# The first microseconds of an attention and gated-layer kernel: w_in loaded by row halves, contiguous copies of turned q, copies of turned k over two banks

## Chip, cores and metric

The kernel runs on one core of a Trainium2 chip. The metric is the device time of one execution in microseconds (us), as the median of several executions; the profile's span is some 1.8 us shorter than that time.

## The reference

```python
def attention(q, k, v):              # 8 batches, 8 heads, 576 tokens, 64 wide; chunks of 64 tokens
    scores = q_chunk @ k_chunk.T / 8
    return softmax(scores) @ v_chunk
def layers(x, w_in, w_out, beta):    # x: 4608 tokens x 512; w_in 512 x 2048; w_out 2048 x 512
    h = x @ w_in
    return (h * sigmoid(beta * h)) @ w_out
# x is the attention's output with the heads side by side
```

## The kernel before

The work is cut into nine blocks of 512 tokens. In a block q and k are cast to bf16 and turned, TensorE forms scores of 64 by 64, ScalarE the exponentials (E), TensorE the product with v, VectorE the normalized x (`x_sb`), which is turned to `xT`. Then follow the first layer (16 tiles of 128 features, tile t in PSUM bank t % 4 of F), tanh and product (`tt`, `g`), and the second layer. The attention of a block is woven into the second layer of the block before it. Blocks 0 and 1 turn q, k and x on TensorE and copy them out of PSUM; from block 2 on transposing transfers issued by SyncE do it. Each engine runs its own list in the order of the times given to `at(...)`.

The parts that the argument touches (cuts marked with `# ...`):

```python
def load_w_in(e0, n):                       # 256 columns of w_in, all 512 rows: runs of 1 KB
    a = w_in[:, 256 * e0:256 * e0 + 256 * n].rearrange("(c p) f -> p c f", p=128)
    # ... issued by SyncE into wstage

def turn_half(blk, name, half, ps, bank, eng):          # blocks 0 and 1
    mid = ps[:, bank, :].bitcast(BF16)
    for i in range(8):
        # ... TensorE turns cast[name][:, c:c + 128] into mid[:, 128 * i:128 * i + 128]
    copy(eng, turned[name][:, :, 256 * half:256 * half + 256].rearrange("x h (p i) -> x h p i", i=8),
         mid.rearrange("x (i p h) -> x h p i", i=8, h=4), ...)      # 1024 elements, read at a step of 4

def scores_half(blk, half, bank0):                      # 32 matmuls of 64 columns
    # ...
    e.matmul(A[64 * c2:64 * c2 + 64, bank0 + h2, col:col + 64],
             turned["k"][r, hp, t], turned["q"][r, hp, t])          # t: 64 neighbouring elements

def exp_half(blk, half, h2, bank0):
    P.op("act", lambda e: e.activation(E[:, 2 * half + h2, :], A[:, bank0 + h2, :], AF.Exp, scale=0.125), ...)

def turn_x(blk, m):                                     # blocks 2 and later
    P.dma("sp", lambda e: e.dma_start_transpose(xT[:, :, 128 * m:128 * m + 128], x_sb[:, m, :]), ...)

at(-99.2, spin, 11, A, 3)                               # warming matmuls, 512 columns each
# ... block 0: tiles 0 and 1 of the first layer in two halves of 256 tokens, tile 2 and later whole
```

The softmax here doesn't subtract the row's maximum and nothing guards it: scores larger than these inputs give would overflow.

Of the kernel before, what the change touches and what calls it, by code (L numbers as in the profile page):

```python
# [11 lines left out]
def K(*key, v=0):  # L12

    return key, v
# [144 lines left out]
def bass_chunk_attention__then__act_swish_beta_kernel(nc, q, k, v, w_in, w_out, beta, out):  # L159
# [7 lines left out]
    with ExitStack() as es:  # L167
# [64 lines left out]
        def halve_beta():  # L232
            for i in range(2):
                P.op("dve", lambda e, i=i: e.transpose(beta_turned[:, i, :], beta_raw[:, i::2]),
                     reads=[K("beta_raw", g) for g in range(4)], writes=[K("beta_turned", i)])
            P.op("pool", lambda e: e.tensor_single_scalar(
                beta_half[:, :, :], beta_turned[:, :, 0:8].rearrange("p i e -> p e i"), 0.5, ALU.mult),
                reads=[K("beta_turned", i) for i in range(2)], writes=[K("beta_half")])


        def load_w_in(e0, n):
            s, at = e0 // 2, 256 * (e0 % 2)
            w = 256 * n

            def f(e):
                a = w_in[:, 256 * e0:256 * e0 + w].rearrange("(c p) f -> p c f", p=128)
                return e.dma_start(
                    wstage[:, s, :].rearrange("p (c f) -> p c f", c=4)[:, :, at:at + w], a)
            P.dma("sp", f, writes=[K("ws", s, e, v=("i", e)) for e in range(e0 % 2, e0 % 2 + n)])

        def cast_w_in(e0, n, engines):
            s, at, w = e0 // 2, 256 * (e0 % 2), 256 * n
            per = 4 // len(engines)
            st = wstage[:, s, :].rearrange("p (c f) -> p c f", c=4)
            for i, eng in enumerate(engines):
                c = slice(per * i, per * i + per)
                dst, src = w_in_bf[:, c, 256 * e0:256 * e0 + w], st[:, c, at:at + w]
                r = [K("ws", s, e, v=("i", e)) for e in range(e0 % 2, e0 % 2 + n)]
                wr = [K("w_in", e0 + x, cc) for x in range(n) for cc in range(4)[c]]
                copy(eng, dst, src, r, wr)  # L260

        def copy(eng, dst, src, r, wr):
            if eng == "act":
                P.op("act", lambda e: e.activation(dst, src, AF.Copy), reads=r, writes=wr)
            else:
                P.op(eng, lambda e: e.tensor_copy(dst, src), reads=r, writes=wr)  # L266
# [75 lines left out]
            copy(eng, dst, src, [K(name + "stage", blk, 2 * half + j, 0, v=blk) for j in range(2)],  # L342
                 [K(name + "cast", 2 * half + j, v=blk) for j in range(2)])

        def turn_half(blk, name, half, ps, bank, eng):
            key = K(*pkey(ps, bank), v=("turn", blk, name, half))
            mid = ps[:, bank, :].bitcast(BF16)
            for i in range(8):
                c = 1024 * half + 128 * i
                P.op("pe", lambda e, i=i, c=c: e.transpose(  # L350
                    mid[:, 128 * i:128 * i + 128], cast[name][:, c:c + 128], identity[:, :]),
                    reads=[K("identity")] + [K(name + "cast", 2 * half + x, v=blk) for x in range(2)],
                    writes=[key])
            copy(eng, turned[name][:, :, 256 * half:256 * half + 256].rearrange("x h (p i) -> x h p i", i=8),
                 mid.rearrange("x (i p h) -> x h p i", i=8, h=4),
                 [key], [K(name + "T", hp, half, v=blk) for hp in range(4)])

        def scores_half(blk, half, bank0):
            for hp in range(4):
                for m in (2 * half, 2 * half + 1):  # L360
                    for h2, c2 in ((0, 0), (1, 1), (0, 1), (1, 0)):
                        col = (2 * hp + m % 2) * 64

                        def f(e, hp=hp, h2=h2, c2=c2, col=col, m=m):
                            r = slice(64 * h2, 64 * h2 + 64)
                            t = slice(64 * (2 * m + c2), 64 * (2 * m + c2) + 64)
                            return e.matmul(A[64 * c2:64 * c2 + 64, bank0 + h2, col:col + 64],
                                            turned["k"][r, hp, t], turned["q"][r, hp, t])
                        P.op("pe", f, reads=[K("qT", hp, half, v=blk), K("kT", hp, half, v=blk)],
                             writes=[K("A", bank0 + h2, v=("s", blk))])  # L370

        def exp_half(blk, half, h2, bank0):
# [3 lines left out]
        def pkey(ps, bank):  # L376
            return "A" if ps is A else "F", bank
# [22 lines left out]
        EB = wstage[:, 0, :].bitcast(BF16).rearrange("k (g x) -> k g x", x=128)  # L400

        def clear_E():
            P.op("pool", lambda e: e.memset(EB, 0.0), writes=[K("ws", 0, e, v="E") for e in range(2)] +
                 [K("EB", u, c2) for u in range(2) for c2 in range(2)])

        def exp(blk, u, c2):
# [79 lines left out]
        def gate(blk, t):  # L486
            bank, T, e0, i = t % 4, NT * blk + t, t // 2, t % 2
            P.op("act", lambda e: e.activation(tt[:, T % NTT, :], F[:, bank, :], AF.Tanh,  # L488
                                               scale=beta_half[:, e0, i:i + 1]),
                 reads=[K("F", bank, v=("h", T)), K("beta_half")], writes=[K("tt", T % NTT, v=T)])  # L490
            P.op("dve", lambda e: e.scalar_tensor_tensor(  # L491
                g2[:, t, :], tt[:, T % NTT, :], 1.0, F[:, bank, :], ALU.add, ALU.mult),
                reads=[K("F", bank, v=("h", T)), K("tt", T % NTT, v=T)], writes=[K("g", t, half, v=blk) for half in range(2)])


        def mm1_pair(blk, pair, half, bank, n, tiles=(0, 1)):
# [66 lines left out]
        def at(time, fn, *args):  # L563
            events.append((time, len(events), fn, args))
# [50 lines left out]
        at(-98.9, load_beta)  # L615
        for m in range(4):
            at(-97.9, load, 0, "v", m)
        at(-99.2, spin, 11, A, 3)
        for e0, n in [(i, 1) for i in range(6)] + [(6, 2)]:
            at(-97.7, load_w_in, e0, n)  # L620
        for j in range(4):
            at(-97.6, load_w_out, j)
        for half in range(2):
# [1 line left out]
                at(-97.5, load_half, 1, name, half)  # L625
        for m in range(4):
            at(-97.4, load, 1, "v", m)
        for t, name, half, cast_eng, turn_t, bank, eng in (
                (4, "q", 0, "dve", 4.7, 0, "act"), (4.1, "k", 0, "dve", 6, 1, "dve"),
                (6.5, "q", 1, "pool", 7.9, 2, "act"), (6.6, "k", 1, "dve", 8.3, 3, "dve")):  # L630
            at(t - 100, cast_half, 0, name, half, cast_eng)
            at(turn_t - 100, turn_half, 0, name, half, F, bank, eng)
        for half, t, t2 in ((0, 8, 8.05), (1, 9.7, 9.75)):
            at(t - 100, scores_half, 0, half, 2 * half)
            for h2 in range(2):
# [1 line left out]
        for m in range(4):  # L637
            at(m - 91.4 if m < 3 else -88.65, cast_v, 0, m, "pool" if m < 3 else "dve")
        for m, t, t2, ps, bank, xb, eng in ((0, 9.2, 11.1, F, 0, 2, "act"), (1, 10, 11.35, A, 0, 3, "act"),
                                            (2, 11.3, 13.5, A, 2, 2, "act"), (3, 12.6, 16.5, A, 0, 3, "dve")):  # L640
            for u in range(2):
                at(t - 100, attend, 0, m, u, ps, bank + u)
            at(t + 0.1 - 100, normalize, 0, m, (0, 1), ps, bank)
            at(t2 - 100, turn_x_pe, 0, m, F, xb, eng)
        for t, n, ps, bank in ((8.35, 2, F, 1), (10.5, 1, F, 3), (11.11, 2, F, 1), (11.4, 1, F, 1),
                               (12.9, 2, F, 1)):
            at(t - 100, spin, n, ps, bank)
        at(8.2 - 100, halve_beta)
        at(13 - 100, cast_w_in, 0, 1, ("pool", "act"))
        at(-83.2, cast_w_in, 1, 1, ("dve", "pool"))  # L650
        for e0 in range(2, 8):
            at(2 * e0 - 2.5, cast_w_in, e0, 1, ("pool", "pool"))
        for j in range(4):
            at(15 + 3 * j, cast_w_out, j, ("pool", "pool"))
        for name, half, ceng, tc, tt_, bank, eng in (
                ("q", 0, "dve", 24, 26.1, 0, "act"), ("k", 0, "dve", 25, 27, 1, "act"),
                ("q", 1, "pool", 26, 29, 2, "dve"), ("k", 1, "pool", 27, 29.9, 3, "act")):
            at(tc, cast_half, 1, name, half, ceng)
            at(tt_, turn_half, 1, name, half, A, bank, eng)
        for half, ts in ((0, 28.95), (1, 30.93)):  # L660
            at(ts, scores_half, 1, half, 2 * half)
            for h2 in range(2):
# [1 line left out]
        for m, ta, ps, bank, tx, xps, xb, eng in (  # L664
# [5 lines left out]
            at(ta + 0.01, normalize, 1, m, (0, 1), ps, bank)  # L670
            at(tx, turn_x_pe, 1, m, xps, xb, eng)

        at(40, clear_E)
        for blk in range(2, NB):
            prepare(blk, 32 * blk - 16)
            attention(blk, 32 * blk - 16)
        for blk in range(NB):
            for n in range(16):
                if n < (2, 6)[blk] if blk < 2 else False:
                    pair, half = (n % (1, 3)[blk], n // (1, 3)[blk])  # L680
                    a = (pair, half, n % 4, n)
                    for i in range(2):
                        at((-84 + 1.05 * i, -82.9)[n] if blk == 0 else 32 * blk + n, mm1_pair, blk, *a, (i,))
                    at((-82.95, 0.9)[n] if blk == 0 else 32 * blk + n + 0.88, gate_pair, blk, *a)
                else:
                    at(32 * blk + n, mm1, blk, n)
                    at(32 * blk + n + 0.05 + 0.9 * (blk == 1), gate, blk, n)
                s, part = (n // 4, n % 4) if blk else (n % 4, n // 4) if n < 8 else \
# [64 lines left out]
```

## Time and profile before

| | before |
|---|---|
| time, median (lowest to highest) | 290.38 us (290.19 to 291.29), 3 runs |
| span of the profiled run | 288.4 us |
| TensorE busy | 278.3 us, 96% of the span |
| second layer of block 0 starts | 31.52 us |
| each block from the third on | 29.49 us |

In the profile lines PE is TensorE, ACT ScalarE, DVE VectorE, POOL GpSimd and SP SyncE; a q behind the name (SPq, ACTq) is the engine's sequencer issuing a transfer; L with a number is a line of the kernel, x with a number how many instructions are taken together, and to turn is to transpose. An issue is the instruction that starts a transfer; the transfer lands later.

The lines that carry the prediction stand in it. Two stages that it does not show matter later. The first is the attention of block 1, woven into the second layer of block 0. This is TensorE's list of work there: start, us from the first start to the last end, line, what, count.

```profile
43.73 0.44 PE L367 MATMUL A<-qT,kT 64*64 64x64 bf16 x32
...
47.59 0.42 PE L367 MATMUL A<-qT,kT 64*64 64x64 bf16 x28
...
49.94 1.05 PE L499 MATMUL F<-xT,w_in_bf 128*128 128x256 bf16 x8
```

A group of 32 scores takes 0.44 us, and the first layer of block 1 begins at 49.94 us. The second stage is the hand-over of x in block 3: SyncE issues four transposing transfers from 101.53 us on, and TensorE goes from the second layer (L523) into the first layer (L479) with no break. SyncE's list, then the chain in order of time:

```profile
101.53 5.49 SPq L453 DMA_TRANSPOSE xT<-x_sb  x4
```

```profile
104.05 6.04 PE F L523 x28
110.09 2.16 PE F L479 x10
```

### The profile page before, as it was taken

What the parts mean: (1) busy time and instruction counts of PE and PEld (TensorE: products, weight loads), DVE (VectorE), ACT (ScalarE), POOL (GpSimd) and SP (SyncE); (2) the same over time, 40 slices, a digit from 0 to 9 for tenths busy, and PEclk for the clock granted to TensorE, in tenths of its full rate; (3) what the DMA queues carried; (4) which work ended last, traced back from release to release, by engine and by line L of the source; (5) the groups of instructions that cost most, each with busy time, mean ns of one, the idle gap of its engine ahead of it and who ended that gap; (6) DMA issues with size and microseconds to landing.
All of it is one profiled execution on the core that took longest, in us unless ns stands there. A gap on an engine that the chain in (4) does not pass through costs nothing.

```text
span 288.4 us, 5455 instructions
## 1 busy us (share of the span) xinstructions
PE 278.3 (96%) x2208; PEld 140.4 (49%) x2243; DVE 148.7 (52%) x292; ACT 161.5 (56%) x233; POOL 77.4 (27%) x115
## 2 busy tenths in 40 slices
PE   5899999999999999999999999999999999999995
PEld 1654456745444544455445544554445444544444
DVE  0777436784348444844384527451856185608601
ACT  2477326877167815882588247834783387438510
POOL 1436854823230622150206020410224020000000
PEclk9799999999999999999999999999999999999999
DMA  6999999999899999895999599958989990340033
GB/s 228 262 350 395 404 332 286 248 178 246 149 273 193 275 203 236 190 232 147 239 222 195 134 237 214 222 112 206 212 165 188 208 226 2 80 135 6 0 71 74
DMA packets 134183, 57.50 MB, mean 199 GB/s; under 512 B 116624, under 2 KB 126096, under 8 KB 134160
## 3 DMA queue, kind: packets, MB, share of 16 engines
q1 hardware_dynamic: 128560, 47.33, 74.4%
q10 hardware_dynamic: 5600, 9.84, 11.2%
q8 instruction: 17, 0.28, 0.4%
q14 instruction: 6, 0.05, 0.1%
HBM read 36.71 MB, written 9.44 MB: 160 GB/s over the span
## 4 chain that ended last, share of the span: by engine, by line
PE 87%; DMA 6%; SPq 3%; issue 1%; DVE 1%; POOL 1%; POOLq 0%
PE F L523 39%; PE F L479 36%; PE A L420 2%; PE F L499 2%; DMA kstage<-in_k_dram 2%; DMA vstage<-in_v_dram 2%; DMA qstage<-in_q_dram 2%; PE A L394 2%; PE F L548 1%; SPq L306 1%; SPq L287 1%; PE F L350 1%; SPq L453 1%; PE A L350 1%; SPq L333 1%
## 5 line engine op out<-in xcount | busy, mean ns | idle before, releaser
L491 DVE SCALAR_TENSOR_TENSOR g<-tt,F 128x512 bf16<-128x512 bf16 x136 | 93.5, 687 | 71.5 <-ACT tt L488 71.3
L523 PE MATMUL F<-w_out_bf,g 128*128 128x512 bf16 x542 | 124.9, 379 | 1.7 <-issue 1.0
L479 PE MATMUL F<-xT,w_in_bf 128*128 128x512 bf16 x527 | 117.9, 379 | 0.9
L488 ACT ACTIVATE tt<-F,beta_half 128x512 bf16<-128x512 f32 x136 | 93.4, 687 | 24.5 <-PE F L479 24.3
L479 PEld LDWEIGHTS F<-xT,w_in_bf 128*128 128x128 bf16 x544 | 53.1, 98 | 64.1 <-DVE g L491 0.5
L523 PEld LDWEIGHTS F<-w_out_bf,g 128*128 128x128 bf16 x560 | 52.1, 98 | 57.3 <-POOL w_out_bf L266 0.3
L531 ACT ACTIVATE ostage<-F 128x512 f32<-128x512 f32 x33 | 19.6, 598 | 67.1 <-PE F L523 66.9
L266 POOL CAST vaug<-vstage 128x512 bf16<-128x512 f32 x35 | 21.5, 613 | 75.9 <-DMA vstage<-in_v_dram 72.1
L415 ACT ACTIVATE wstage<-A 64x1024 bf16<-64x1024 f32 x28 | 28.5, 1018 | 5.2 <-PE A L394 4.7
L266 POOL CAST qcast<-qstage 128x1024 bf16<-128x1024 f32 (+1 forms) x18 | 17.0, 945 | 44.8 <-DMA qstage<-in_q_dram 44.2
L446 DVE TENSOR_TENSOR x_sb<-A,rden 128x256 bf16<-128x256 f32 (+1 forms) x62 | 27.9, 450 | 2.1
L444 DVE RECIPROCAL rden<-A 128x4 f32<-128x4 f32 (+1 forms) x62 | 11.1, 179 | 30.6 <-PE A L420 29.4
L266 POOL CAST kcast<-kstage 128x512 bf16<-128x512 f32 (+1 forms) x29 | 18.1, 628 | 25.1 <-DMA kstage<-in_k_dram 24.8
L420 PEld LDWEIGHTS A<-vaug,wstage 128*128 128x128 bf16 x224 | 10.8, 98 | 6.6
L420 PE MATMUL A<-vaug,wstage 128*128 128x65 bf16 x224 | 11.7, 193 | 0.0
L266 POOL CAST w_in_bf<-wstage 128x512 bf16<-128x512 f32 x14 | 8.2, 613 | 7.5 <-DMA wstage<-in_moe_w_in_dram 7.5
L266 POOL CAST w_out_bf<-wstage 128x1024 bf16<-128x1024 f32 x8 | 8.1, 1040 | 1.9 <-DMA wstage<-in_moe_w_out_dram 1.9
L266 DVE CAST qcast<-qstage 128x1024 bf16<-128x1024 f32 x2 | 1.9, 934 | 12.6 <-DMA qstage<-in_q_dram 12.6
L499 PE MATMUL F<-xT,w_in_bf 128*128 128x256 bf16 x64 | 8.0, 273 | 0.2
L509 ACT ACTIVATE tt<-F,beta_half 128x256 bf16<-128x256 f32 x16 | 6.7, 470 | 2.2 <-PE F L499 2.1
L553 DVE TENSOR_SCALAR ostage<-F 128x256 f32<-128x256 f32 x2 | 0.8, 424 | 12.0 <-PE F L548 12.0
L513 DVE SCALAR_TENSOR_TENSOR g<-tt,F 128x512 bf16<-128x512 bf16 x8 | 5.5, 686 | 2.2 <-ACT tt L509 2.2
(58 smaller groups left out, 88.8 us busy)
## 6 DMA issues: line engine op xcount, KB each, us to landing
vstage<-in_v_dram SPq DMA_DIRECT2D x32, 256.0 KB, 5.2
out_dram<-ostage ACTq DMA_DIRECT2D x32, 256.0 KB, 3.4
kstage<-in_k_dram SPq DMA_DIRECT2D x30, 256.0 KB, 6.5
qstage<-in_q_dram SPq DMA_DIRECT2D x12, 512.0 KB, 5.4
wstage<-in_moe_w_out_dram SPq DMA_DIRECT2D x4, 1024.0 KB, 12.9
wstage<-in_moe_w_in_dram SPq DMA_DIRECT2D x6, 512.0 KB, 8.1
qstage<-in_q_dram SPq DMA_DIRECT2D x8, 256.0 KB, 8.6
wstage<-in_moe_w_in_dram SPq DMA_DIRECT2D x1, 1024.0 KB, 11.0
```

The costliest lines, as they stand in the source:

```text
L266: P.op(eng, lambda e: e.tensor_copy(dst, src), reads=r, writes=wr)
L415: P.op("act", lambda e: e.activation(dst, src, AF.Exp, scale=0.125), reads=[K("A", 2 * u + i, v=("s", blk)) for i in range(2)], writes=[K( ...
L420: P.op("pe", lambda e, h=h: e.matmul(A[:, bank, 128 * (h % 4):128 * (h % 4) + 65], EB[:, 16 * u + 8 * (h % 2) + 4 * (h // 2 % 2) + m, :], ...
L444: P.op("dve", lambda e: e.reciprocal(rd, o[:, :, :, 64]), reads=r, writes=[K("rden", m, u, v=blk) for u in us])
L446: P.op("dve", lambda e: e.tensor_tensor(x_sb[:, m, 256 * us[0]:256 * (us[0] + n)].rearrange("p (b h d) -> p b h d", h=4, b=n), o[:, :, :, ...
L479: P.op("pe", lambda e, c=c: e.matmul(F[:, bank, :], w_in_bf[:, c, 256 * e0 + i:256 * e0 + 256:2], xT[:, c, :], start=(c == 0), stop=(c == ...
L488: P.op("act", lambda e: e.activation(tt[:, T % NTT, :], F[:, bank, :], AF.Tanh, scale=beta_half[:, e0, i:i + 1]), reads=[K("F", bank, v=(" ...
L491: P.op("dve", lambda e: e.scalar_tensor_tensor(g2[:, t, :], tt[:, T % NTT, :], 1.0, F[:, bank, :], ALU.add, ALU.mult), reads=[K("F", bank, ...
L499: P.op("pe", lambda e, i=i, c=c: e.matmul(F[:, bank, 256 * i:256 * i + 256], w_in_bf[:, c, 256 * pair + i:256 * pair + 256:2], xT[:, c, 25 ...
L509: P.op("act", lambda e, i=i: e.activation(tt[:, s, 256 * i:256 * i + 256], F[:, bank, 256 * i:256 * i + 256], AF.Tanh, scale=beta_half[:, ...
L523: P.op("pe", lambda e, t=t: e.matmul(F[:, s, :], g2[:, t, 128 * s:128 * s + 128], w_out_bf[:, t, :], start=(t == 0), stop=(t == NT - 1)), ...
L531: f = (lambda e: e.activation(dst, src, AF.Copy, scale=0.5)) if eng == "act" else \
```

## The change

The intent is to shorten the first 20 us, while TensorE waits for data. w_in of block 0 comes in 2 KB runs (256 rows of 512 columns per load) for 1 KB runs. As a load then holds half the rows of four tiles, the first four tiles are summed as 256-token halves in all eight PSUM banks, two row chunks at a time. Turned q is copied contiguously, and the scores read it with a step instead. In block 0 turned k is written to two banks and copied by VectorE and ScalarE together. There are 14 warming matmuls for 11. Smaller moves go with this: the first half of turned q is copied by VectorE for ScalarE, and two copies of turned x use other banks. The core of the diff:

```diff
-            a = w_in[:, 256 * e0:256 * e0 + w].rearrange("(c p) f -> p c f", p=128)
+            a = w_in[128 * c0:128 * (c0 + n), 512 * s:512 * s + 512].rearrange("(c p) f -> p c f", p=128)
...
-        def turn_half(blk, name, half, ps, bank, eng):
+        def turn_half(blk, name, half, *parts):
...
+                if name == "q":
+                    copy(eng, turned["q"][:, 2 * half:2 * half + 2, :].rearrange("x a t -> x (a t)"), mid, ...)
+                else:
+                    copy(eng, turned["k"][...].rearrange("x h (p i) -> x h p i", i=8)[:, :, :, n * j:n * j + n],
+                         mid.rearrange("x (i p h) -> x h p i", i=n, h=4), ...)
...
+                            p = 8 * (2 * m + c2 - 4 * half)
+                            qq = turned["q"][r, 2 * half:2 * half + 2, :].rearrange(
+                                "x a (i p h) -> x h p (a i)", i=4, h=4)[:, hp, p:p + 8]
-                                            turned["k"][r, hp, t], turned["q"][r, hp, t])
+                                            turned["k"][r, hp, t], qq)
...
+        def mm1_half(blk, t, half, ps, cs=range(4)):    # 256 tokens of tile t, row chunks cs
+        def gate_half(blk, t, half, ps):
...
-        at(-99.2, spin, 11, A, 3)
+        at(-99.2, spin, 14, A, 3)
...
-                (4, "q", 0, "dve", 4.7, 0, "act"), (4.1, "k", 0, "dve", 6, 1, "dve"),
-                (6.5, "q", 1, "pool", 7.9, 2, "act"), (6.6, "k", 1, "dve", 8.3, 3, "dve")):
+                (4, "q", 0, "dve", 4.7, (F, 0, "dve")), (4.1, "k", 0, "dve", 6, (F, 1, "dve"), (A, 2, "act")),
+                (6.5, "q", 1, "pool", 7.9, (F, 2, "act")), (6.6, "k", 1, "dve", 8.3, (F, 3, "dve"), (A, 2, "act"))):
...
+        for t in range(4):
+            for cp in range(2):
+                for half in range(2):
+                    at(16 + 2 * cp + half + 0.1 * t - 100, mm1_half, 0, t, half, (F, A)[half], (2 * cp, 2 * cp + 1))
```

`turn_half` and `scores_half` serve block 1 as well, so the new q copy and the new reading are in force there too.

## The prediction

> **What bounds the kernel now.** I read the page's chain first, then the chain of waits of the first 40 us in order of time, then what GpSimd waits for, then the clock by 3.4 us stretches.
>
> The chain that ended last, shares of the span by engine:
>
> ```profile
> PE 87%; DMA 6%; SPq 3%; issue 1%; DVE 1%; POOL 1%; POOLq 0%
> ```
>
> TensorE is the chain. From 60 us on each block of 32 tile sums takes the same 29.49 us (the chain's L479 piece of 10.74 us starts at 82.81, 112.30, 171.29, 200.78), and start-to-start distances of the matmuls show no gap beyond missing records. So nothing after the first block can be gained by this change; the end moves by as much as the dense stretch moves. Where does it begin? The chain, start, us, what:
>
> ```profile
> 9.38 1.03 PE F L350 x8
> 10.41 0.62 PE A L367 x19
> 11.03 1.01 PE F L350 x8
> 12.04 0.02 issue
> 12.06 1.23 DVE kT L266
> 13.30 0.04 issue
> 13.34 0.45 PE A L367 x32
> ...
> 17.14 0.44 PE F L499 x4
> 17.58 0.26 PE F L462 x4
> 17.84 0.02 issue
> 17.86 0.43 DVE xT L266
> 18.30 0.05 issue
> 18.34 1.05 PE F L499 x8
> 19.39 0.05 issue
> 19.44 10.95 PE F L479 x49
> ```
>
> At 12.06 to 13.30 the scores of the second half wait for the copy of turned k; at 17.86 the last copy of turned x is awaited. From 18.34 TensorE is dense: tile 4 of the first layer starts at 18.34 + 8x0.108 + 8x0.216 = 20.93, the second layer at 31.52. Next, whether w_in is close behind. GpSimd, start, us, then what ended its idle time:
>
> ```profile
> 16.08 0.61 POOL L266 CAST w_in_bf<-wstage 128x512 bf16<-128x512 f32 x1 [2.18 <-DMA wstage<-in_moe_w_in_dram]
> 17.55 0.61 POOL L266 CAST w_in_bf<-wstage 128x512 bf16<-128x512 f32 x1 [0.85 <-DMA wstage<-in_moe_w_in_dram]
> 20.04 1.17 POOL L266 CAST w_in_bf<-wstage 128x512 bf16<-128x512 f32 x2 [1.88 <-DMA wstage<-in_moe_w_in_dram]
> 21.55 1.17 POOL L266 CAST w_in_bf<-wstage 128x512 bf16<-128x512 f32 x2 [0.34 <-DMA wstage<-in_moe_w_in_dram]
> ```
>
> It is very close. Loads 1, 2, 3, 4 of w_in (512 KB each) land at 16.03, 17.49, 19.99, 21.50 by the trace's completion records. The casts of load 3 end at 20.65 and 21.21, and tile 4 needs them at 20.93 and 21.36: 0.15 us to spare. One real stall, 0.2 us at 28.0, is the wait for the last load's cast. Load 3 is a full 1.0 us late against the 1.5 us rhythm: in the completion records 15 engines finish it by 18.97 and one at 19.99; that engine stays 1.0 us behind in loads 4 to 7. In the stretch from 16 to 17 us stands the reason I assume, a fetch of instructions on another queue:
>
> ```profile
> q8 instruction: 1, 0.02, 7.0%
> ```
>
> 7.0% of 16 engines over 1 us is 1.1 us of one engine.
>
> **What the Trainium skill says.** "VectorE: DVE Perf Modes", section "Mode 2×_1P — pack two bf16 into one 32-bit read": two results a cycle for 16-bit data with unit step. The trace agrees: the copy of turned x (512 bf16, unit step, from PSUM) takes 0.42 us, that of turned k (1024 bf16, step 4) 1.23 us. "DMA: Bandwidth & Descriptors", section "Why small descriptors are slow (HBM only)": a fixed cost per packet. Here 1 KB runs give 512 KB in 1.50 us (loads 3 to 6), 2 KB runs 1.36 (load 7: 1 MB in 2.71), 4 KB runs 1.28 (w_out: 1 MB in 2.56). "TensorE: Matmul & The Clock Gate", section "What's actually happening": the array falls to half rate after an idle window of about 3.4 us. The trace is sterner: the clock fell although 46% of the window was busy. Stretch, PE busy, weight loads, DVE, ACT, POOL, clock, DMA share, GB/s:
>
> ```profile
> 5.06:8.48 3.42, 1.56 (x16) 0.80 (x15) 1.29 (x2) 0.20 (x1) 0.19 (x1) 1.00 1.02 358
> 8.48:11.89 3.41, 3.10 (x56) 2.50 (x54) 2.04 (x4) 2.26 (x4) 1.50 (x3) 0.50 1.29 238
> 11.89:15.30 3.41, 2.98 (x91) 1.84 (x88) 3.13 (x6) 1.95 (x5) 1.38 (x3) 1.00 1.09 270
> ```
>
> **The change part by part.**
>
> Three more warming matmuls (14 for 11). At full clock 3x0.216 = 0.65 us, ending near 6.4 instead of 5.8, well before the first turn at 7.62. The window 5.06 to 8.48 becomes (1.56+0.65)/3.42 = 65% busy. I expect, at 2 in 3, that the clock then holds. A group of eight turns falls from 1.03 to about 0.5 us and scores from 0.62 to 0.45.
>
> Turned copies. From the two durations above a stepped copy costs 0.16 + 1.04 ns an element, a contiguous one half per element: q on VectorE 0.16 + 1024x0.52 ns = 0.69 us, against 1.02 on ScalarE. k over two banks: 512 elements in 0.69 on VectorE beside 0.60 on ScalarE (its 512-element copy of x), against 1.23. With a held clock: q at 8.28 to 8.97, k at 8.97 to 9.66; second half's q turned from 9.38 (GpSimd's cast ends 9.34, unchanged) to 9.9, scores to 10.4. ScalarE then has q (1.02), two exponentials (0.54 each) and its half of k (0.60) in that order: 9.95 + 1.02 + 1.08 + 0.60 = 12.65. Scores of the second half start near 12.7 instead of 13.34, a gain of 0.6; with the half clock 13.2, a gain of 0.15. The q reading of the scores gets a step of four elements; 128 such matmuls of about 14 ns each are too few to matter.
>
> First four tiles. 32 matmuls of 256 for 16 of 256 and 8 of 512: 32x0.108 = 3.46 against 3.45 us. No cost. Tanh is 8x0.42 for 4x0.42 + 2x0.69, the products on VectorE alike, still under TensorE's pace.
>
> When do they run? Load 1 lands at 16.03 - 0.14 = 15.9, casts of its two row chunks end at 16.5 on both engines (ScalarE is now free when it lands; before it started at 16.33). First four matmuls 16.6 to 17.04, the last turn of x, four more to 17.7; last copy of x by 17.9 (before 18.29). Then 24 matmuls of 0.108: tile 4 could start at 17.94 + 2.59 = 20.5, 0.4 us earlier than now.
>
> But loads. Tile 4 now needs loads 3 and 4 at once: both row halves of the second stripe. Before it needed load 3 only, and load 4 waited until tile 6, 1.7 us later. The four loads gain 4x0.14 = 0.56 us. With the late engine as before load 4 lands at about 21.50 - 0.6 = 20.9; GpSimd casts chunks 2 and 3 one after the other, 1.17 us, to 22.1. Tile 4's fourth matmul is wanted at 21.15 and runs at 22.1: a stall of 0.95. Tile 4 ends at 22.3; 11 tiles of 0.863 follow, 31.8 for the second layer against 31.52. The 0.2 us stall at 28.0 goes (the last load lands near 26.3), which is in this sum. w_out lands 0.8 us sooner and is hidden.
>
> Sum: about +0.25 us, 290.6.
>
> **The rivals.** (a) The late engine is not late: the instruction fetch comes at another time or strikes less. Load 4 lands at 19.9, its casts end at 21.1, no stall to speak of. Then the second layer starts at 20.5 + 12x0.863 = 30.9, 0.6 us earlier: 289.8. For it: the fetch is one event and hangs on where the instruction stream stands. Against: the programs hardly differ in instructions before 16 us. If instead it strikes an engine that already trails (they spread over 1.1 us), load 4 is up to 1 us later still: 291.5. (b) The stall at tile 4 throttles the clock: 1.0 us idle in a window of 3.4 is 70% busy, above the 46% that tripped it. If it trips, 3.4 us at half speed cost 1.7: 292.3. I give it one in ten. (c) The attention start becomes the bound because the clock falls anyway: it moves tile 4 from 20.5 to about 20.9, still before the cast at 22.1, so it adds nothing.
>
> **Range and chances.** The stall on load 4 at 6 in 10 (290.6), no stall at 3 in 10 (289.8), throttling or a later load at 1 in 10. I say 290.4, 289.5 to 291.6. Two per cent are 5.8 us; the whole start holds no such gain, and a loss of that size would need two throttled windows.
>
> **What would show it.** Right: GpSimd's second cast pair after load 4 ends near 22.1 and TensorE has its only gap there, inside tile 4; w_in loads 1.36 us apart except one; scores' second half near 12.7; clock 1.00 from 8.5 to 11.9. Wrong: tile 4 runs through without a gap, or the dense stretch starts later than 17.9 by another wait, or a copy of turned k is still what the second scores wait for on VectorE rather than on ScalarE.

## The result, and the profile after

The kernel after takes 292.99 us (292.58 to 293.57, 6 runs), against 290.30 us of before (289.88 to 291.29, 6 runs). The ratio is 1.0087, with a 95% interval of 1.0067 to 1.0107; a ratio here is the mean time of one kernel's fast runs over that of the other's of the same rounds, so not quite the ratio of the medians. That is slower, by less than 2%, and 1.4 us above the upper end of the predicted range. The span of the profiled run is 291.3 us, 2.9 more.

The page's chain of the kernel after has a new member: SyncE's queue (SPq) holds 5% for 3%.

```profile
PE 87%; SPq 5%; DMA 4%; ACT 1%; DVE 1%; ACTq 1%; POOL 0%; issue 0%
```

Where the 2.9 us come in is read best from four landmarks on TensorE. M0 is the start of the second layer of block 0; M1, M2 and M3 are the starts of the last unbroken 28 matmuls in the second layers of blocks 1, 2 and 3 (the 104.05 of the chain above is M2; by TensorE's list it is 103.89).

| | M0 | M0 to M1 | M1 to M2 | M2 to M3 | span |
|---|---|---|---|---|---|
| before | 31.52 | 42.88 | 29.49 | 29.49 | 288.4 |
| after | 31.98 | 44.48 | 29.62 | 30.22 | 291.3 |
| difference | +0.46 | +1.60 | +0.13 | +0.73 | +2.9 |

From M3 on the two kernels agree within 0.03 us. So there are three places. The first is the one that the prediction was about. The chain after, in order of time:

```profile
12.52 8.45 DMA wstage<-in_moe_w_in_dram
20.97 0.05 issue
21.02 1.18 POOL w_in_bf L260 x2
22.21 0.05 issue
22.25 1.90 PE F L487 x8
```

Load 4 of w_in lands at 20.97, GpSimd casts its two row chunks until 22.2, and the last matmul of tile 4 waits for that. The second place is block 1. TensorE's list after, to be read beside the three lines of before:

```profile
44.19 1.07 PE L374 MATMUL A<-qT,kT 64*64 64x64 bf16 x32
...
48.68 1.06 PE L374 MATMUL A<-qT,kT 64*64 64x64 bf16 x30
...
51.67 1.05 PE L528 MATMUL F<-xT,w_in_bf 128*128 128x256 bf16 x8
```

Both groups of scores take 1.06 us for 0.44, and the first layer of block 1 begins 1.73 us later than before, of which 0.46 are inherited. A further 0.33 us is lost a little later, where the chain now leaves TensorE:

```profile
49.80 1.08 ACT E L381 x2
50.88 0.99 ACT ostage L560 x2
51.86 0.02 issue
51.88 1.66 ACTq L567
53.54 0.05 issue
53.59 0.86 ACT tt L538 x2
```

The later scores put the exponentials, two evictions and the issues of two stores behind each other on ScalarE, in front of the first tanh of block 1, and the issue of the second store takes 1.66 us, where in before it took 0.34. The third place is the start of block 3:

```profile
106.50 0.43 DVE x_sb L454
106.93 2.30 SPq L461
109.23 0.06 issue
109.29 3.42 DMA xT<-x_sb
112.71 0.14 issue
112.84 2.32 PE F L487 x10
```

SyncE needed 2.30 us to issue the third of four transposing transfers of x, where before it took 1.39; the fourth was issued late, landed at 112.71, and TensorE stood still for 0.7 us. The chain names the issue, but the transfers were late as well. From issue to landing, least, median and most of the four, first before, then after:

```profile
DMA to landing us min/median/max: 2.5/3.5/4.3
DMA to landing us min/median/max: 3.4/4.9/6.0
```

The most is the first transfer's in both. In the kernel after, the issue of this first transfer ended at 105.58, before the slow third issue, and yet it landed at 109.90, 6.04 us after its issue began, for 4.26 in before. In the stretch from 107 to 109 us the list of DMA queues shows one packet of the instruction queue:

```profile
q8 instruction: 1, 0.02, 4.5%
```

### The profile page after: what moved, and what is told of

It reads as the page before. It is cut to its first block, busy times and chain, and to the rows that moved or that the text cites. A ratio compares the mean times of both kernels' runs of the same rounds, so it can differ in the third digit from the quotient of the medians.

```text
span 291.3 us, 5526 instructions
## 1 busy us (share of the span) xinstructions
PE 283.6 (97%) x2254; PEld 142.6 (49%) x2254; DVE 148.5 (51%) x297; ACT 161.6 (55%) x236; POOL 77.5 (27%) x115
## 4 chain that ended last, share of the span: by engine, by line
PE 87%; SPq 5%; DMA 4%; ACT 1%; DVE 1%; ACTq 1%; POOL 0%; issue 0%
PE F L487 40%; PE F L552 39%; DMA wstage<-in_moe_w_in_dram 3%; PE A L428 2%; SPq L281 2%; PE A L402 2%; SPq L327 1%; PE F L577 1%; DMA xT<-x_sb 1%; PE F L528 1%; SPq L461 1%; SPq L246 1%; PE A L374 1%; PE A L346 1%; ACTq L567 1%; POOL w_in_bf L260 0%
## 5 line engine op out<-in xcount | busy, mean ns | idle before, releaser
L499 DVE SCALAR_TENSOR_TENSOR g<-tt,F 128x512 bf16<-128x512 bf16 x134 | 92.2, 688 | 72.0 <-ACT tt L496 71.8
L552 PE MATMUL F<-w_out_bf,g 128*128 128x512 bf16 x560 | 128.5, 379 | 0.0
L496 ACT ACTIVATE tt<-F,beta_half 128x512 bf16<-128x512 f32 x134 | 92.1, 687 | 24.8 <-PE F L487 24.6
L487 PEld LDWEIGHTS F<-xT,w_in_bf 128*128 128x128 bf16 x536 | 52.2, 98 | 64.5 <-issue 1.5
L479 PE MATMUL A<-identity 128*128 128x512 bf16 x14 | 5.3, 564 | 1.5 <-POOL identity L217 1.5
L381 ACT ACTIVATE E<-A 128x512 bf16<-128x512 f32 x8 | 4.3, 594 | 4.1 <-PE A L374 4.1
L402 PEld LDWEIGHTS A<-qT,kT 64*64 64x64 bf16 x448 | 4.8, 106 | 3.0 <-issue 3.0
```

What stands on the lines that cost most here:

```text
L402: return e.matmul(A[64 * c2:64 * c2 + 64, bank, col:col + 64], turned["k"][r, hp, t], qq)
L487: P.op("pe", lambda e, c=c: e.matmul(F[:, bank, :], w_in_bf[:, c, 256 * e0 + i:256 * e0 + 256:2], xT[:, c, :], start=(c == 0), stop=(c == ...
L496: P.op("act", lambda e: e.activation(tt[:, T % NTT, :], F[:, bank, :], AF.Tanh, scale=beta_half[:, e0, i:i + 1]), reads=[K("F", bank, v=(" ...
L499: P.op("dve", lambda e: e.scalar_tensor_tensor(g2[:, t, :], tt[:, T % NTT, :], 1.0, F[:, bank, :], ALU.add, ALU.mult), reads=[K("F", bank, ...
L552: P.op("pe", lambda e, t=t: e.matmul(F[:, s, :], g2[:, t, 128 * s:128 * s + 128], w_out_bf[:, t, :], start=(t == 0), stop=(t == NT - 1)), ...
```

## The experiments

Sixteen kernels ran, all with correct results. Theory S says that the loss in block 1 is the stepped reading of q by TensorE; theory F says that the loss before blocks 2 and 3 comes from a fetch of instructions that falls on the issue of SyncE's transposing transfers; the main rival W says that the loss behind the gate of load 4 comes from the new order of w_in, because the loads of later blocks then run earlier and get in the way of other transfers. A fetch of instructions is one packet of 16 KB on the queue "q8 instruction". The landmarks of the profiled runs are given together here; "1 look" is a single run.

| kernel | time us | ratio to before [95%] | M0 | M0 to M1 | M1 to M2 | M2 to M3 |
|---|---|---|---|---|---|---|
| q_old_block1 | 291.61 | 1.0053 [1.0019, 1.0086] | 33.59 | 42.87 | 29.49 | 30.55 |
| q_old_both | 291.23 | 1.0031 [1.0006, 1.0055] | 31.97 | 42.88 | 29.49 | 30.16 |
| before_q_new | 291.88 | 1.0059 [1.0024, 1.0094] | 31.71 | 44.15 | 29.49 | 29.49 |
| before_w_in_new | 291.48 | 1.0036 [1.0014, 1.0057] | 31.95 | 42.87 | 29.74 | 29.49 |
| before_k_warm | 291.08 | 1.0007 [0.9956, 1.0057] | 31.35 | 42.87 | 29.50 | 29.71 |
| q_step8 | 308.59 | 1.0596 [1.0535, 1.0657] | 40.22 | 53.14 | 29.49 | 29.89 |
| q_step8_reads | 292.19 | 1.0068 [1.0039, 1.0097] | 33.24 | 43.26 | 29.50 | 30.38 |
| two_tiles | 291.19 | 1.0005 [0.9957, 1.0054] | 31.18 | 42.88 | 29.49 | 29.87 |
| two_tiles_q_step8 | 308.25 | 1.0593 [1.0539, 1.0647] | 38.83 | 52.22 | 29.68 | 30.68 |
| two_tiles_q_step8_reads | 292.17 | 1.0085 [1.0045, 1.0125] | 31.19 | 43.26 | 29.49 | 30.62 |
| two_tiles_no_warm | 290.52 (1 look) | | 31.71 | 42.87 | 29.50 | 29.49 |
| two_tiles_80_tiny | 292.88 (1 look) | | 34.01 | 42.94 | 29.49 | 29.68 |
| after_9_warm | 293.11 | 1.0083 [1.0049, 1.0117] | 32.21 | 44.18 | 29.49 | 30.59 |
| two_tiles_9_warm | 291.56 | 1.0036 [0.9996, 1.0075] | 32.06 | 42.87 | 29.49 | 30.05 |
| two_tiles_no_warm_timed | 291.94 | 1.0042 [0.9996, 1.0087] | 32.38 | 43.04 | 29.69 | 30.44 |
| after_no_warm | 292.79 | 1.0069 [1.0026, 1.0111] | 33.34 | 44.15 | 29.49 | 29.50 |

Before itself had medians of 290.68, 290.37, 290.04, 290.28 and 290.41 us. M0 of a single profile moves by more than a microsecond with how the loads and the clock fall at the start (q_old_block1's profiled run of 293.26 us was the slowest of its four), so M0 is compared with caution; the other columns repeat to 0.01 us where nothing happens.

### The parts, undone and done alone

q_old_block1: the kernel after with the old copy and the contiguous reading of q in block 1 only (cuts marked with `...`, here and in the edits below).

```diff
-                if name == "q":
+                if name == "q" and blk == 0:
...
+                            if not (blk == 0):
+                                qq = turned["q"][r, hp, t]
```

> The changed kernel, but block 1 copies turned q in the old stepped way and its scores read q contiguously; block 0 keeps the new form. Theory S (the new read of q makes each score matmul cost about 31 ns instead of 14, and in block 1 TensorE is dense, so 64 of them cost 1.1 us, plus some 0.3 to 0.5 us of waits that follow): 1.1 to 1.6 us faster than the changed kernel, about 291.6. Rival W (the loss after the stall on load 4 comes from the loads of later blocks running earlier, so that the transposing DMAs and the stores get in each other's way): within 0.3 us of the changed kernel, 292.7 to 293.2.

Measured: ratio 1.0053 for 1.0087. M0 to M1 is 42.87 for 44.48: the whole 1.6 us of block 1 are gone. The profiled run had a late start, so its M0 says nothing.

q_old_both: the same in both blocks.

```diff
-                if name == "q":
+                if name == "q" and False:
...
+                            if not (False):
+                                qq = turned["q"][r, hp, t]
```

> As the run before, with the old q form in block 0 too (copy on the same engines as in the changed kernel: VectorE first half, ScalarE second). Theory S: block 0's scores shrink by 0.5 us each, but the first tiles wait for w_in, so the same as q_old_block1 within 0.3 us, about 291.6. Rival W: 292.7 to 293.2.

Measured: ratio 1.0031, M0 to M1 42.88. TensorE's list of this kernel:

```profile
44.18 0.45 PE L376 MATMUL A<-qT,kT 64*64 64x64 bf16 x32
```

The new order of w_in is still in this kernel and block 1 loses nothing, so the loss there is not W's but goes with q. What is left to before lies at M0 (+0.45), the gate that both theories have, and between M2 and M3 (+0.67), which W could still explain.

before_q_new: the kernel before with the new q copy and reading only, which are the q lines of the diff above.

> The kernel before with only the new form of q (contiguous copy, stepped read in the scores) in both blocks, all else as before. Theory S: block 1 costs 1.1 us, block 0 has its start on the path as well (scores of the second half sit right before the dense stretch), another 0.3 to 0.5: 291.5 to 292. Rival W: no w_in change, so within 0.3 us of 290.3.

Measured: ratio 1.0059, with scores of 1.07 us and M0 to M1 of 44.15. So the reading of q costs 1.27 us in block 1 by itself, with no change to w_in at all. The other 0.33 us of the kernel after (the store's issue of 1.66 us on ScalarE) are not there: here that issue takes 0.34 us. Nothing is lost between M1 and M3 in this kernel.

before_w_in_new: the kernel before with the w_in part only (loads, casts, mm1_half, gate_half of the diff).

> The kernel before with only the new w_in (2 KB runs by row halves, first four tiles as 256-token sums in eight banks); 11 warming matmuls, q and k copies as before. Both theories: tile 4 waits for load 4's casts near 22.2, second layer starts near 32.0 instead of 31.5. Theory S: that is all, 290.6 to 290.9. Rival W: 292 or more.

Measured: ratio 1.0036; M0 +0.43, M0 to M1 as before, and 0.25 us between M1 and M2. The median of 291.48 is 0.6 us above what S expected and below what W expected; the profiled run was the fastest of the four (290.90). The w_in part costs its gate and something before block 2, a stage with no transfer of w_in.

before_k_warm: the kernel before with k over two banks and 14 warming matmuls.

```diff
-        at(-99.2, spin, 11, A, 3)
+        at(-99.2, spin, 14, A, 3)
...
-                (4, "q", 0, "dve", 4.7, 0, "act"), (4.1, "k", 0, "dve", 6, 1, "dve"),
+                (4, "q", 0, "dve", 4.7, (F, 0, "act")), (4.1, "k", 0, "dve", 6, (F, 1, "dve"), (A, 2, "act")),
...
```

> The kernel before with only k's turned copies over two banks and 14 warming matmuls. The scores of the second half start 0.5 us earlier; but tile 4 is then held by the casts of load 3 (21.2), so the second layer starts at most 0.3 us earlier: 290.0 to 290.5. If these parts carry a loss of their own: 291 or more.

Measured: ratio 1.0007, not to be told from before. The interval is wide (one run of before took 292.90), and the median of 291.08 lies where the expectation put a loss of these parts' own, so a loss of some tenths is not excluded. M0 was 0.17 us earlier, and 0.22 us were lost between M2 and M3. The three parts alone sum to 1.0102 in ratio against 1.0087 measured, so within their intervals they add up.

### The step of the reading

The inner step of the new reading is not four elements. TensorE reads the 64 columns as p outside and (a, i) inside: the inner step is 128 elements, 256 bytes, and only the outer one is four elements. "SBUF — State Buffer" of the Trainium skill, section "Door 1: The DMA port swizzle", says that SBUF has cachelines of 16 bytes and that "each access that crosses to a new line pays a penalty". A reading with the 8-byte step inside crosses half as often: two elements share a line, by the addresses, where at 256 bytes each has its own.

q_step8: the same contiguous copy, the reading with the 8-byte step inside, and the exponential undoing the order as it writes E.

```diff
-                                "x a (i p h) -> x h p (a i)", i=4, h=4)[:, hp, p:p + 8]
+                                "x a (i p h) -> x h (a i) p", i=4, h=4)[:, hp, :, p:p + 8]
...
+                E[:, 2 * half + h2, :].rearrange("k (g p i) -> k g i p", p=8, i=8),
+                A[:, bank0 + h2, :].rearrange("k (g i p) -> k g i p", p=8, i=8), AF.Exp, scale=0.125),
```

> The changed kernel, its contiguous q copy kept, but the scores read q with 8-byte steps inside (8 elements) and 256-byte steps outside, instead of the other way round; the exponential writes its result back in token order, so the output is right. If the inner step of 256 bytes is what slows the read: a score matmul at 14 to 16 ns start to start instead of 25 to 31, block 1 gets back its 1.1 us, 291.3 to 291.7 in all. If any stepped read in two levels is slow: 31 ns and 292.7 to 293.2 as the changed kernel.

Measured: 308.59 us. The scores did become shorter (0.63 us a group), but the exponentials that write bf16 elements 16 bytes apart took 2.33 us each for 0.54, which I had not reckoned with:

```profile
10.74 4.66 ACT L381 ACTIVATE E<-A 128x512 bf16<-128x512 f32 x2
```

q_step8_reads: the exponential walks in the order of its output, so that the step falls on its reading of PSUM.

```diff
-                E[:, 2 * half + h2, :].rearrange("k (g p i) -> k g i p", p=8, i=8),
-                A[:, bank0 + h2, :].rearrange("k (g i p) -> k g i p", p=8, i=8), AF.Exp, scale=0.125),
+                E[:, 2 * half + h2, :].rearrange("k (g p i) -> k g p i", p=8, i=8),
+                A[:, bank0 + h2, :].rearrange("k (g i p) -> k g p i", p=8, i=8), AF.Exp, scale=0.125),
```

> As q_step8, but the exponential walks in the order of its output, so that it writes runs of 64 and reads PSUM in steps (in q_step8 it wrote bf16 elements 16 bytes apart and took 2.33 us instead of 0.54). If the scattered writing alone was the cause: exponentials of 0.54 us, scores of 0.40 us a group as in q_step8, and the whole 291.3 to 291.8, 1.3 us under the changed kernel. If reading PSUM in steps of 32 bytes is as slow: above 300.

Measured: ratio 1.0068, and 292.19 us is above the expected 291.3 to 291.8: the scores did not reach the 0.40 us of the expectation, and the profiled run lost 0.88 us between M2 and M3. The exponentials are back at 0.54 us, M0 to M1 is 43.26, and the scores:

```profile
45.45 0.63 PE L374 MATMUL A<-qT,kT 64*64 64x64 bf16 x32
```

So a group of 32 scores takes 0.44 us at unit step, 0.63 at a step of 8 bytes, 1.07 at 256 bytes, with the same arithmetic, and M0 to M1 follows in the same order: 42.88, 43.26, 44.15. With that S is shown by doing, undoing and sizing. Why a step costs what it costs is not: half the crossings left 0.19 of the 0.63 us, less than a third, so the count of crossings alone does not give the sizes. Even the better step loses 0.38 us in block 1.

### The gate of load 4

two_tiles: q_old_both with tiles 4 and 5 interleaved by row halves, so that tile 5's first half fills the wait for load 4.

```diff
...
+                elif blk == 0 and n in (4, 5):
+                    at(4 + 0.1 * (n - 4), mm1, 0, n, (0, 1))
+                    at(4.5 + 0.1 * (n - 4), mm1, 0, n, (2, 3))
+                    at(4.55 + 0.1 * (n - 4), gate, 0, n)
```

> q_old_both with tiles 4 and 5 interleaved: first two row chunks of both, then the last two of both, so that the casts of load 4 are wanted 0.43 us later. If the stall inside tile 4 is on the path: gap of about 0.6 us shrinks to 0.2 or less, second layer starts near 31.5 instead of 31.97, and the whole is 0.4 us faster than q_old_both, 290.6 to 290.9. If something behind it takes over (w_in of later stripes, gates): no change, 291.2.

Measured: ratio 1.0005, not to be told from before, though the median of 291.19 is above the expected 290.6 to 290.9; M0 is 31.18, 0.8 us earlier than q_old_both and 0.34 earlier than before. That is a gain of the kind the change was after, though one profile each does not settle its size (before_k_warm had 31.35, and the same edit with 9 warming matmuls, below, 32.06). It is given back by 0.38 us between M2 and M3.

two_tiles_q_step8 and two_tiles_q_step8_reads: both edits together.

> Both repairs on the changed kernel. If both work: as two_tiles, 290.5 to 291.0, at best level with the kernel before. If the inner step is not the cause: 292.3 or more.

> The same with tiles 4 and 5 interleaved. If both hold: 290.3 to 291.0, level with two_tiles.

Measured: 1.0593, by the same slow exponentials, and 1.0085, with 292.17 us for the expected 290.3 to 291.0. The latter's profiled run had M0 at 31.19 and M0 to M1 at 43.26, as its parts promise, but lost 1.13 us between M2 and M3.

### The wait before block 3

In the kernel after the instruction fetch in question begins at 107.4 us, on top of the third issue (106.93 to 109.23). In before it begins at 111.3 us, after the last issue has ended at 107.02. two_tiles_no_warm is two_tiles without the warming matmuls, which takes 28 TensorE instructions (matmuls and weight loads) out ahead of everything.

```diff
-        at(-99.2, spin, 14, A, 3)
```

> two_tiles without the 14 warming matmuls: 28 TensorE instructions fewer ahead of everything, to move the instruction fetches of the later blocks. In the traces so far 20 of 36 issues of a transposing DMA for x that overlapped a fetch took over 1.5 us instead of 1.27, and 4 of 132 that did not. Theory F (a fetch that falls on block 3's transposes delays them, which makes TensorE wait before block 3): where the fetch near 104.5 us no longer overlaps them, they take 1.27 us each and the gap before block 3 (0.38 us in two_tiles) is gone; where it still overlaps, one stays over 1.9. Rival L (the w_in order itself brings the k loads of SyncE too close): one of the four stays slow whether a fetch overlaps or not, gap 0.2 to 0.7 us.

Measured: 290.52 us in one look. The fetch came at 111.6 us for 104.5 in two_tiles, the four issues took 1.62, 1.26, 1.39 and 1.26 us, and M2 to M3 was 29.49: no wait.

two_tiles_80_tiny: 80 matmuls of 8 columns in place of the 14.

```diff
...
-        at(-99.2, spin, 14, A, 3)
+        at(-99.2, tiny, 80)
```

> two_tiles with 80 tiny matmuls (8 columns) in place of the 14 warming ones: 132 TensorE instructions more ahead of everything. Theory F: fetches come some microseconds earlier in each block; block 3's transposes are slow only if one overlaps them. Rival L: as in the run without warming, slow all the same.

Measured: 292.88 us, mostly by a clock that stayed low at the start (M0 34.01). The fetches lay at 102.5 and 121.5 us, off the issues, and M2 to M3 was 29.68; the small loss follows a first issue of 1.84 us that no fetch met.

after_9_warm: the kernel after with 9 warming matmuls, to move that fetch alone.

```diff
-        at(-99.2, spin, 14, A, 3)
+        at(-99.2, spin, 9, A, 3)
```

> The kernel after with 9 warming matmuls for 14, so ten TensorE instructions fewer ahead of everything and nothing else. In two_tiles_no_warm 28 fewer moved the fetch of instructions that sits at 104.5 us to 111.6, 0.25 us per instruction. Theory F (a fetch on top of SyncE's transposing transfer of x makes the issue longer, and block 3 waits): the fetch that sits at 107.4 us moves to about 110, behind the last of the four issues (ends about 109.4), they take 1.25 to 1.6 us each, the 0.72 us gap before block 3 goes, and the time is about 0.7 us below the kernel after's 293.0: 292.3, ratio to before 1.0065. The fetch at 75.1 us moves to about 77.6 and still meets an issue of block 2, so the 0.14 us there may stay. Rival (the gap comes from where x lands, or from the longer scores that push SyncE's queue, not from the fetch): the gap stays near 0.7 us and the ratio near 1.0087. A fallen clock at the start could add up to 0.3 us to either.

Measured: a miss. The fetch moved to 108.6 us only, where I had reckoned 110, and there it met the fourth issue (108.26 us), which took 1.82 us; M2 to M3 rose to 30.59. My rule of 0.25 us per instruction was wrong, and the ratio of 1.0083 is that of the kernel after.

two_tiles_9_warm, the same edit to two_tiles, and two_tiles_no_warm_timed, two_tiles_no_warm once more:

> two_tiles with 9 warming matmuls for 14. It has the old q reading, the new order of w_in and tiles 4 and 5 interleaved by row halves. Theory F: the fetch at 104.5 us moves to about 107, the transposing transfers of x of block 3 are issued in 1.25 to 1.6 us each, the gap of 0.38 us goes: about 0.3 us under the time before, ratio 0.999. Rival: gap and ratio (1.0005) as in two_tiles.

> The kernel of two_tiles_no_warm once more, timed, to see whether its one look of 290.52 us stands: by theory F its first layer is some 0.5 us later than two_tiles's (clock cold at the start) and its block 3 0.38 us earlier, so about 291.2, ratio 1.0010. If the cold clock cost nothing, 290.0.

Measured: in two_tiles_9_warm the fetch (107.0 us) met the fourth issue (106.47, 1.97 us), and 0.56 us were lost: another miss, the ratio is 1.0036 for the expected 0.999. two_tiles_no_warm_timed had a median of 291.94 us, so the single look of 290.52 did not stand; its profiled run lost 0.95 us between M2 and M3 with no fetch on the four issues. There the k loads ahead of them on SyncE ran late, the first issue began 0.57 us after its x was ready, and took 2.19 us, and the fourth transfer landed 3.77 us after its issue began, for 2.54 in before. That run speaks against F as the only cause, and for rival L of the expectations, the k loads.

after_no_warm: the kernel after without the warming matmuls.

```diff
-        at(-99.2, spin, 14, A, 3)
```

> The kernel after without the warming matmuls, 28 TensorE instructions fewer. after_9_warm (10 fewer) moved the fetch at 107.4 us only to 108.6, not to 110 as I wrote, and there it met the fourth issue of the transposing transfers of x: that issue took 1.82 us and the gap before block 3 grew from 0.72 to 1.10 us. In two_tiles 28 fewer moved it by 7.1 us. Theory F: the fetch lies near 114 us, the second to fourth issue take 1.25 to 1.45 us each, and the gap before block 3 is 0.3 us or less. Where the start of the first layer is not later than in the kernel after by more than 0.5 us (the clock is cold until some 14 us, but the gate of load 4 hides a part), the time is 292.5 to 293.0, ratio about 1.008. Rival: the gap does not hang on the fetch; in two_tiles_no_warm_timed it was 0.95 us without any overlap, after a first issue of 2.19 us that the issues of the k loads had held back. Then the gap is 0.7 us or more with second to fourth issues of normal length.

Measured: the fetch lay at 114.7 us, the issues took 1.70, 1.26, 1.42 and 1.25 us, and M2 to M3 was 29.50 for 30.22 in the kernel after. In the same profiled run, however, another fetch of 1.8 us fell on the third issue of block 7, at 225.9 us; the issue took 2.91 us in all (2.27 of them after its x was ready), and the same chain appeared there:

```profile
225.37 0.43 DVE x_sb L454
225.81 2.27 SPq L461
228.08 0.04 issue
228.12 4.06 DMA xT<-x_sb
232.19 0.14 issue
232.32 3.83 PE F L487 x17
```

It cost 1.3 us, and this run was the slowest of its four (294.55 us, median 292.79). The wait left the block that the fetch left, and came to the block that the fetch came to. The 0.33 us of block 1 went too (M0 to M1 is 44.15), and they go with a fetch as well: in the kernel after one begins at 51.8 us, on the store's issue of 1.66 us at 51.88; in after_9_warm at 51.7, and the issue at 52.12 took 1.35; in before_q_new and here the fetches lie at 53.5 and 53.3 us, after the issue, which took 0.34 and 0.40. Over all 18 traces none of the 641 store issues clear of a fetch took more than 0.65 us; but of the 79 that met one only nine took more than 0.8, so a fetch does not always do it.

Of the transposing issues for x the 18 traces have 504. Of 104 that overlap a fetch 54 took more than 1.5 us, of the 400 others 17, and 16 of those 17 were the first issue of block 3, right behind the k loads on SyncE's queue. "Runtime: NRT & Kernel Launch" of the Trainium skill, section "Instruction fetch mechanics", calls the cost of crossing a 16 KiB boundary of the instruction stream "mostly hidden". Here a fetch of 16 KB keeps a DMA engine busy for 0.9 to 1.4 us in most cases (2.7 in the longest of 318), and what is late with it are transfers that SyncE and ScalarE had issued.

The completion records say more than the issues. In block 3 eight of the nine traces whose fetch began 3.3 to 3.8 us after the first issue had the first transfer land 5.7 to 6.3 us after that issue began; in the six traces with no fetch on the four issues it took 4.3 to 4.7, or 5.4 in two_tiles_no_warm_timed. (The ninth, before_w_in_new, landed its first transfer 0.2 us after the fetch began; its second took 5.4 for the 4.1 of before.) Where the fetch came 4.7 to 5.0 us in (before_k_warm, after_9_warm, two_tiles_9_warm), the first transfer was in time and the second took 5.5 to 5.6 us. ScalarE's store of that stage landed 4.94 us after its issue in the kernel after, for 3.11 in before. So transfers under way are late with a fetch, not only the issue that it meets; and a long issue may itself come of the transfers ahead of it. No run here separates the two.

## Why the prediction was wrong

**The load gate: right.** Load 4 was to land at 20.9, its casts to end at 22.1, the second layer to start at 31.8. Measured: 20.97, 22.2 and 31.98. The stall is where it was predicted, inside tile 4. The term "+0.25" was +0.46: the last matmul of tile 4 ran at 22.25 for 22.1, eleven tiles followed it without a break, and the prediction's own 31.8 less 31.52 is 0.28. That tile 4 began at 21.00 for the predicted 20.5 cost nothing, as the cast was the gate. Part of the fit is luck: load 4 was late by one trailing engine, as assumed, but in this profile that engine or another trailed by 0.83 us in load 1 already (16.29, the next at 15.46), before the fetch at 16.3 that was to be the reason.

**Turned copies and clock: right, without effect.** q took 0.69 us on VectorE, and the scores of the second half began at 12.59 for the predicted 12.7. The clock held from 5.83 us on. But it held as well with 11 warming matmuls in the profiles of before_q_new and before_w_in_new, so the three more are not shown to have done it.

**The failed step: "The q reading of the scores gets a step of four elements; 128 such matmuls of about 14 ns each are too few to matter."** The inner step is 128 elements, not four, which the change's own line says ("p (a i)" puts a and i inside). The duration was taken from contiguous readings of before, 0.45 us for 32, and the reading made it 1.06. And "too few to matter" overlooked where half of them stand: in block 1, where TensorE is dense and every nanosecond is on the path. 64 matmuls in two groups cost 2 x 0.63 = 1.26 us, which is the 1.27 measured in before_q_new. In block 0 the same matmuls did no harm that shows (M0 31.98, and 31.97 with the old form in q_old_both): the gate of load 4 comes later.

**The second failed step: "So nothing after the first block can be gained by this change; the end moves by as much as the dense stretch moves."** The change moves no work there, but the dense blocks have one hand-over with little slack, x through SyncE's queue: the last transfer landed at 108.28 us in before by its completion record, 1.65 us ahead of TensorE's need at 109.93. Measured from M2, the first of the four landed 1.91 us later in the kernel after, the last 2.24, which is more than the slack. A different number of instructions shifts where the fetches fall. The kernel after lost 0.13 and 0.73 us there, before in its profiled run nothing.

The sum as it came: +0.46 (load gate), +1.27 (reading of q), +0.33 (the store's issue on ScalarE under a fetch), +0.86 (hand-over of x), in all 2.9. Of the rivals in the prediction none happened: load 4 was not early, the clock did not fall, and the attention's start did not become the bound.

**What stays open.** That the fetch is what delays the issues and landings is inferred from the overlaps and from the kernels that moved it, and by which of the two TensorE is made to wait is open; why the issue of an unmet first transfer took up to 2.19 us, and the 0.95 us of two_tiles_no_warm_timed with it, is not explained. The link of the 0.33 us to a fetch rests on four traces and was not tested by itself. No kernel here is shown to be faster than before: two_tiles is not to be told from it.

## What to carry to other kernels

When a copy is made contiguous, somebody else reads with the step: find out which engine that is, which index is innermost, and whether that engine is on the path in every place where the code is used. A dense TensorE stretch is only as safe as the slack of its hand-overs, and a change to the number of instructions can move fetches onto them (here inferred, not isolated), so a loss of a few tenths far from the edit is looked for there, in several runs, before it is put down to the edit. A load cut differently is timed by when its last needed part is cast, not by its rate: here filling the wait with the next tile's first half took the second layer of block 0 from 31.97 to 31.18 us in one pair of profiles; the run times do not show it as a gain.

## What the Trainium skill lacked or had wrong

- "SBUF — State Buffer" has the penalty for crossing a 16-byte line, but no figure and not that TensorE's moving operand feels it, and it lets one stride "for free" up to 8 bf16. Here 32 score matmuls of 64 columns took 0.44 us at unit step, 0.63 us with runs of eight elements at a step of 4 bf16 (and a jump of 256 bytes between runs) and 1.07 us at a step of 128 elements. The middle pattern stays below a step of 8 bf16 within its runs and is not free; how much of it is the jumps was not measured.
- "Runtime: NRT & Kernel Launch" calls the cost of a fetch mostly hidden. It says nothing there of transfers on other queues. Here 54 of the 104 transposing issues that overlapped one took over 1.5 us for some 1.27 (17 of 400 others), the first transfer of block 3 took 5.7 to 6.3 us to land in eight traces with a fetch on it, 4.3 to 4.7 in five of the six without, and after one fetch TensorE stood for 1.3 us. The cause is inferred.
- No page that I used has a figure for ScalarE's scattered write: exponentials of 128 x 512 into bf16 elements 16 bytes apart took 2.33 us, contiguous 0.54; with the step on the reading of PSUM it was 0.54.
- "DMA: Bandwidth & Descriptors" has a fixed cost per packet, worked out for 256 bytes, but no measured time at these lengths: 512 KB took 1.50 us in 1 KB runs, 1.36 in 2 KB, 1.28 in 4 KB.
- "TensorE: Matmul & The Clock Gate" speaks of an idle window; here the clock fell after a window that was 46% busy. With the 18 traces cut into windows of 3.41 us at the changes of the granted clock, the full clock fell after windows in which TensorE was busy for 47% or less, and was kept after all those of 47% or more.
